# Delta-rule attention ahead of two expert layers: whole-tile key loads, side-by-side key copies on ScalarE, key masks behind the first solve, all late evictions on ScalarE

## The chip, the cores and the metric

One core of a Trainium2 chip runs the whole program. The metric is the device time of one execution in microseconds (us), lower is better. TensorE (PE) multiplies matrices, VectorE (DVE), ScalarE (ACT) and GpSimd (POOL) work elementwise, SyncE (SP) issues most of the transfers. TensorE's granted clock is 1.00 or 0.50 of full speed (2.4 or 1.2 GHz) in every row of a single stretch; a stretch that mixes both shows a value between.

## The reference, cut to what matters

```python
def _attn_ref(q, k, v, beta):            # (2, 8, 768, 48), beta (2, 8, 768)
    k_n = k / (np.linalg.norm(k, axis=-1, keepdims=True) + 1e-06)
    state = np.zeros((B, H, D, D))
    for t in range(S):
        y[:, :, t] = einsum('bhd,bhde->bhe', q[:, :, t], state)
        v_old = einsum('bhde,bhd->bhe', state, k_n[:, :, t])
        state = state + beta_t * einsum('bhd,bhe->bhde', k_n[:, :, t], v[:, :, t] - v_old)
...
    x = attn_out.transpose(0, 2, 1, 3).reshape(B * S, H * D)     # 1536 x 384
    x = _moe_ref(x=x, **moe_kwargs)        # top-1 expert of 8, 384 -> 1024 -> 384, relu
    return _moe2_ref(x=x, **moe2_kwargs)   # a second such layer, with an output gate
```

The attention has a state that each token changes. The two expert layers behind it send every token through one of eight experts.

## The kernel before

The 768 tokens of each of the 16 heads are cut into 24 chunks of 32 tokens (`NCH`), and four chunks make a group (`NQ` = 6). The work on all heads of a chunk goes together. A chunk's tokens act on one another through a triangular system, so its inverse is needed before the state can take the chunk in. `inlane` (L588) makes the inverses for a batch of chunks at once, one step per row of the triangle: `BATCH` is 4, 4, 8 and 8 chunks. The batches are called solve 1 to 4 below. Solves 1, 3 and 4 run on DVE (a product L706 and a subtraction L708 per step: 15 such pairs in solve 1, 31 in solves 3 and 4), solve 2 on POOL.

A solve begins with the Gram products of its chunks (`gram`, L524; matmuls L543 for group 0, L537 for the others) in halves `h` of two chunks. L537 has a key tile `kq` as one operand and, as the other, a tile `kb` in which the keys of the two batch halves stand side by side with zeros between. Before, both are loaded from memory: `load_k` (L447) loads `kq` of groups 1 to 5 in two transfers of 48 partitions, into tiles that DVE and ACT have set to zero (L1073 to L1079), and `load_kb` (L461) loads the same numbers again, twice 48 partitions, into `kb`, which POOL has set to zero (L1070). Each half of a Gram product has a PSUM buffer of the ring `R` (two buffers), which is read twice: by ACT for the solve (L560, `Ge`, into `Gs`) and by DVE for the mask of the query part (L566, `Pe`, into `PT`), and is free for the next user after both.

After a solve its result is spread into `zt` by DVE (L747), ACT (L745) and transfers (L749). In solves 1 and 2 the chunks are corrected by `fix` (L772): matmul f1 (L782), transposition on DVE (L786), matmul f2 (L793), four ACT evictions (L798). Then the recurrence runs, `step(c)` (L822), with these matmuls in each chunk: AT (L835), U (L845), AS (L850), QS (L864), DS (L870), PW (L885). AS needs the state of the chunk before it. From AS on the chain goes: four evictions of `wpd` (L857 on ACT or L855 on DVE), DS, two evictions of the state `sbd` (L878 on ACT or L876 on DVE), AS of the next chunk. Chunks 0 to 15 evict on ACT, chunks 16 to 23 in turn on ACT and DVE (`WENG`, `SENG`, L900). `logits` and `route` follow the chunks, and the expert layers follow the attention.

No engine chooses its order on the chip. `Plan` (L221) sorts all operations of the attention by estimated times and ranks and writes one fixed order per engine; an instruction that waits holds all that stand behind it on its engine. `keep_warm` (L380) adds matmuls without use (`warm`, L820) where the planner thinks TensorE too idle to keep its clock; `NW0` (L1122) more stand at the start. Loads go out on SP in the order of the list in L1060.

```python
        add(("Ge", q, h), "A", 0.38, lambda h=h: e1(h), ((hd, 1),) + ...
        add(("Pe", q, h), "V", 0.5, lambda h=h: e2(h), ((hd, 1), "bl") + ...
        WENG, SENG = ("AAAA", "AA") if c < 16 else ("AVAV", "VA")
```

Of the kernel before, what the change touches and what calls it, by code (L numbers as in the profile page):

```python
# [7 lines left out]
F32 = mybir.dt.float32  # L8
# [212 lines left out]
class Plan:  # L221
# [169 lines left out]


def attention(tc, ctx, con, I, C, wg, A, xt1, xa1, xt2, zr, T1, Ti1, place, load_w, late, wts, xb, new_x, gather):
# [6 lines left out]
    starts = [sum(BATCH[:i]) for i in range(NB)]  # L400
    bof = lambda c: max(j for j in range(NB) if starts[j] <= c)
    pl = Plan()
    pl.bufs.update(Lt=1, Zt=1, kb=2, kq=10, kt=4, vt=3, PT=5, R=2, WA=2, O=1, ATn=2, pay=4, lgs=2, Gs=1, Bl=3, z=1, ztmp=1, xTs=1, sq=1, f1s=4, Gw=2)
    P = 4.3
    GP = 0.0021
    add = pl.add
    rest = lambda c: (NCH - c) * P
# [12 lines left out]
    kbb = [big.tile([128, 2, 2, 8, 64], F32, name=f"kb{i}") for i in range(2)]  # L420
    wab = [ps.tile([128, 512], F32, name=f"WA{i}") for i in range(2)]
    Sps = ps.tile([128, 2, 4, 48], F32, name="Sps")
    zps = ps.tile([128, 512], F32, name="zps")
    T, st = {}, {}
    GR = ((0, 1), (2, 3), (4,), (5,))
    gof = {q: g[0] for g in GR for q in g}
# [16 lines left out]
    def chain(key, xfer, f, new=None, uses=(), n=1, deps=()):  # L443
        dma(key, xfer, f, deps, behind=order[-1:], new=new, uses=uses, n=n)
        order.append(key)

    def load_k(q, h):  # L447
        i = slice(2 * h, 2 * h + 2)

        def f(e):  # L450
            t = T["kqt", q, h] = kqb[(2 * q + h) % len(kqb)]
            src = I["kq"][:, 4 * q + i.start : 4 * q + i.stop]
            if q == 0:
                e.dma_start(t, src)
# [4 lines left out]
        chain(("kq", q, h), 1.46 if q == 0 else 1.1, f, new=("kq", ("kqt", q, h)), n=2 if q else 1, deps=(("kz", 2 * q + h),) if 2 <= 2 * q + h < len(kqb) else ())

    def load_kb(q, h):  # L461
        def f(e):
            t = T["kbt", q, h] = kbb[(2 * q + h) % 2]
            src = I["kq"][:, 4 * q + 2 * h : 4 * q + 2 * h + 2]
            for b in range(2):
                e.dma_start(t[64 * b : 64 * b + 48, b], src[64 * b : 64 * b + 48])

        chain(("kb", q, h), 1.1, f, new=("kb", ("kbt", q, h)), n=2, deps=(("bz", h),))

    def load_kt(q, h):  # L470
        i = slice(2 * h, 2 * h + 2)
# [52 lines left out]
    def gram(q, pri=0.0):  # L524
# [37 lines left out]
        def e2(h):  # L562
            if h == 0:
                sb("PT", ("PT", q), [128, 4, 2, 2, 32])
            x, y = parts(h, T["PT", q], 32, 64)
            nc.vector.tensor_tensor(x, y, bl[:, NB].unsqueeze(1).to_broadcast([128, 8, 32]), ALU.mult)  # L566

        for h in range(2):
            hd = ("G", q, h)
            for i in range(2):  # L570
                dp = (("kq", q, h), ("kb", q, h)) if q else (("kq", 0, i),)
                if i:
                    dp += ((hd, 0),)
                elif h:
                    dp += ((("G", q, 0), 1),)
                elif q:
                    dp += ((("G", q - 1, 1), 1),)
                us = (("kqt", q, h), ("kbt", q, h)) if q else (("kqt", 0, i),)
                add((hd, i), "P", 0.4 if q else 0.32, lambda h=h, i=i: mm(h, i), dp, pri, behind=late_, uses=us + ((hd,) if i else ()), new=None if i else ("R", hd))
        for h in range(2):  # L580
            hd = ("G", q, h)
            f0 = starts[b] // 4
            f = q == f0 and h == 0
            add(("Ge", q, h), "A", 0.38, lambda h=h: e1(h), ((hd, 1),) + (() if f else (("Ge", f0, 0),)), pri, uses=(hd,) + (() if f else (("Gs", b),)), new=("Gw" if BATCH[b] == 4 else "Gs", ("Gs", b)) if f else None)
            add(("Pe", q, h), "V", 0.5, lambda h=h: e2(h), ((hd, 1), "bl") + ((("Pe", q, 0),) if h else ()), rest(4 * q + 2 * h) + 12, lp=500.0, uses=(hd,) + ((("PT", q),) if h else ()), new=None if h else ("PT", ("PT", q)))
    ZV = {}

    def inlane(bi):  # L588
# [13 lines left out]

        def z0():
            if psum:
                d["z"] = zps[:, 0:256].rearrange("p (i m) -> p i m", m=16)
            elif blk:
                d["z"] = zzb[:, 0:256].rearrange("p (i m) -> p i m", m=16)
            else:
                d["z"] = sb("z", Z, [128, 32, 32])
            (nc.vector if psum else nc.gpsimd).memset(d["z"], 0.0)  # L610
# [211 lines left out]
    def step(c):  # L822
# [246 lines left out]
    for i in range(2):
        add(("bz", i), "G", 1.9, lambda i=i: nc.gpsimd.memset(kbb[i], 0.0), lp=600.0 - i)  # L1070
    for i, (n, t) in enumerate([("zta0", zt8[:, 0:4]), ("wpd0", wpd[0]), ("sbd1", sbd[1]), ("wpd1", wpd[1]), ("zta1", zt8[:, 4:8]), ("sbd0", sbd[0])]):
        add(n, "G", {"zta0": 1.9, "zta1": 1.9}.get(n, 0.7), lambda t=t: nc.gpsimd.memset(t, 0.0), pri=500 - i)
    for n, (k, t) in enumerate([("Sz", Sps), ("Wz0", wab[0]), ("Wz1", wab[1])] + [(("kz", i), kqb[i]) for i in range(2, len(kqb))]):  # L1073
        kd = n > 2
        if n > 5:
            f = lambda t=t: nc.scalar.activation(t.rearrange("p a b c -> p (a b c)"), nc.const_aps.tensor(0.0, [128, 1024], F32), AF.Copy)
        else:
            f = lambda t=t: nc.vector.memset(t, 0.0)
        add(k, "A" if n > 5 else "V", 1.08 if kd else 0.5, f, pri=1200 - n, after=0.0)  # L1079
# [34 lines left out]
    for j in range(2):  # L1114
# [664 lines left out]
```

## Time and profile before

| | us |
|---|---|
| three runs, median | 553.44 |
| three runs, lowest and highest | 550.39, 555.61 |
| the profiled execution, its time | 550.83 |
| the profiled execution, its span | 549.0 |
| granted TensorE clock over the span | 0.931 of full speed |

The span runs from the first to the last profiled instruction; 1.83 us of the execution lie outside it. Times of rows are counted from the start of the span. The attention ends at about 194.4 us, where the last table for the gathers is written, and the expert layers take the rest. A row of the timeline gives start, duration, engine, line, operation, tiles, count, and in brackets how long the engine had been idle before it and what ended that.

### The profile page before, as it was taken

Reading aid. Unit: us, or ns where it says so; the run is one execution under the profiler, and the core shown is the slowest. Engines: PE = TensorE matmul, PEld = TensorE weight load, DVE = VectorE, ACT = ScalarE, POOL = GpSimd, SP = SyncE. Lnnn points to the kernel's source line nnn. Section 1 sums busy time; section 2 is a strip of 40 time slices with the busy share of each in tenths; the row PEclk is TensorE's granted clock in tenths of the full one; section 3 lists DMA queues with packets and bytes.
Section 4 is the critical chain, followed back from the end, with each engine's and each line's share of the span. In section 5 each row is a group of like instructions: output and inputs, shape, how many; then the busy total and the mean of one; then the engine's idle time right before and its main releaser. Section 6 shows DMA issues by size and latency. Waiting matters only on the chain. (4 is left out here: it accounts for less than half of the span.)

```text
span 549.0 us, 13219 instructions
## 1 busy us (share of the span) xinstructions
PE 482.5 (88%) x5173; PEld 412.8 (75%) x5182; DVE 355.6 (65%) x1042; ACT 275.0 (50%) x597; POOL 136.5 (25%) x161
## 2 busy tenths in 40 slices
PE   8798989799899869999999999999788996898780
PEld 3357767677676539999999999988677895898570
DVE  6566656899255466788788788987236853466550
ACT  6014635646744435675665656644225651445540
POOL 8504100000000055053254141116331513121111
PEclk9896958859999979999999999999999999799897
DMA  8992170353646122857547676433932844335400
GB/s 253 249 241 43 36 213 27 80 153 91 174 111 184 32 63 61 304 180 256 179 130 276 206 233 219 137 88 82 348 98 84 299 176 154 143 99 192 146 11 14
DMA packets 56538, 83.21 MB, mean 152 GB/s; under 512 B 15615, under 2 KB 38359, under 8 KB 56432
## 3 DMA queue, kind: packets, MB, share of 16 engines
q1 hardware_dynamic: 50688, 69.90, 41.8%
q0 software_dynamic: 5744, 11.95, 7.1%
q8 instruction: 59, 0.97, 0.7%
q14 instruction: 47, 0.39, 0.2%
HBM read 72.80 MB, written 11.72 MB: 154 GB/s over the span
## 5 line engine op out<-in xcount | busy, mean ns | idle before, releaser
L1177 DVE TENSOR_TENSOR l<-r,h 128x768 fp32r<-128x768 f32 x128 | 118.1, 952 | 14.8 <-ACT h L1173 12.0
L1173 ACT ACTIVATE h<-r 128x768 fp32r<-128x768 f32 x128 | 101.8, 837 | 3.5 <-DMA xa<-aux 3.5
L1189 PE MATMUL hp<-xh,h 128*128 128x256 f32 x288 | 84.4, 293 | 13.4 <-issue 8.8
L1189 PE MATMUL y<-h,hh 128*128 128x384 f32 x240 | 84.4, 352 | 0.0
L1191 PE MATMUL hp<-xl,h 128*128 128x256 f32 x288 | 81.9, 284 | 0.0
L1190 PE MATMUL hp<-xh,l 128*128 128x256 f32 x288 | 81.8, 284 | 0.0
L1190 PE MATMUL y<-h,hl 128*128 128x384 f32 x240 | 80.9, 337 | 0.0
L1191 PE MATMUL y<-l,hh 128*128 128x384 f32 x240 | 80.7, 336 | 0.0
L1221 ACT ACTIVATE hh<-hp 128x256 fp32r<-128x256 f32 x96 | 36.5, 384 | 67.6 <-PE hp L1191 57.2
L1224 DVE SCALAR_TENSOR_TENSOR hl<-hp,hh 128x256 fp32r<-128x256 f32 x96 | 39.7, 421 | 45.3 <-ACT hh L1221 41.0
L1189 PEld LDWEIGHTS hp<-xh,h 128*128 128x128 f32 x288 | 55.8, 194 | 15.4 <-issue 13.2
L1190 PEld LDWEIGHTS hp<-xh,l 128*128 128x128 f32 x288 | 56.1, 195 | 0.1
L1191 PEld LDWEIGHTS hp<-xl,h 128*128 128x128 f32 x288 | 55.7, 193 | 0.1
L168 POOL DMA_INDIRECT out<-fo,fix x19 | 21.6, 1134 | 109.3 <-DVE fo L1401 77.6
L1190 PEld LDWEIGHTS y<-h,hl 128*128 128x128 f32 x240 | 45.3, 189 | 0.7 <-issue 0.4
L1189 PEld LDWEIGHTS y<-h,hh 128*128 128x128 f32 x240 | 45.2, 188 | 0.0
L1191 PEld LDWEIGHTS y<-l,hh 128*128 128x128 f32 x240 | 45.1, 188 | 0.0
L168 POOL DMA_INDIRECT xt<-p,rix x16 | 16.6, 1036 | 101.6 <-ACT h L1173 72.4
L210 POOL DMA_INDIRECT xb<-xt,Ti x32 | 38.1, 1191 | 12.6 <-issue 6.1
L857 ACT ACTIVATE wpd<-WA 32x192 f32<-32x192 f32 x80 | 25.8, 322 | 18.0 <-PE WA L850 11.1
L1203 ACT ACTIVATE xh<-xp 128x384 fp32r<-128x384 f32 x29 | 14.3, 492 | 40.4 <-PE xp L1200 28.4
L820 PE MATMUL warm<-const-bfloat16-1.0 128*128 128x512 bf16 x93 | 29.0, 444 | 1.4 <-PEq L1772 0.8
(273 smaller groups left out, 881.8 us busy)
## 6 DMA issues: line engine op xcount, KB each, us to landing
r<-moe_w SPq DMA_DIRECT2D x64, 768.0 KB
kq<-kq SPq DMA_DIRECT2D x20, 192.0 KB
kb<-kq SPq DMA_DIRECT2D x20, 192.0 KB
xt<-zr SPq DMA_DIRECT2D x3, 776.0 KB
kt<-ktm SPq DMA_DIRECT2D x12, 192.0 KB
vt<-vtm SPq DMA_DIRECT2D x6, 384.0 KB
xt<-pay SPq DMA_DIRECT2D x16, 96.0 KB
kq<-kq SPq DMA_DIRECT2D x2, 512.0 KB
```

The lines of the kernel that those rows point to most:

```text
L168: i = nc.gpsimd.indirect_dma_start(out=dst, out_offset=IO(ap=idx, axis=0), in_=src, in_offset=None, bounds_check=rows - 1, oob_is_err=False)
L210: nc.gpsimd.indirect_dma_start(out=dst, out_offset=None, in_=src, in_offset=IO(ap=ix, axis=0), bounds_check=1536, oob_is_err=False)
L820: nc.tensor.matmul(t, one_[:, 0:128], one_, start=True, stop=True)
L857: nc.scalar.activation(wp[p, :, Q, :], st["W", c][p], AF.Copy)
L1173: nc.scalar.activation(v(h), v(r), AF.Copy)
L1177: nc.vector.tensor_tensor(v(l), v(r), v(h).bitcast(F32), ALU.subtract)
L1189: nc.tensor.matmul(o, lh, rh, start=first, stop=False)
L1190: nc.tensor.matmul(o, ll, rh, start=False, stop=False)
L1191: nc.tensor.matmul(o, lh, rl, start=False, stop=last)
L1203: nc.scalar.activation(xs()[0][:, :, s], p[0], AF.Copy)
L1221: nc.scalar.activation(hs()[0][:, f], p[0], AF.Relu)
L1224: nc.vector.scalar_tensor_tensor(hs()[1][:, f], p[0], 0.0, hs()[0][:, f].bitcast(F32), ALU.max, ALU.subtract)
```

## The change

```diff
     def keep_warm(self, free, t, d, u):
         k, t0 = 0, t
+        if t < 24:
+            return 0
...
-    pl.bufs.update(Lt=1, Zt=1, kb=2, kq=10, kt=4, vt=3, PT=5, R=2, ...
+    pl.bufs.update(Lt=1, Zt=1, kb=2, kq=10, kt=4, vt=3, PT=5, R=3, ...
+    KA, KL = 3, (0.0, 900.0, 0.0, 0.0)
+    LOADS = "k0 l t0 v0 k1 t1 v1 k2 t2 k3 v2 t3 k4 K4 k5 K5 v3 t4 v4 t5 v5"
...
-    zps = ps.tile([128, 512], F32, name="zps")
...
-            src = I["kq"][:, 4 * q + i.start : 4 * q + i.stop]
-            if q == 0:
-                e.dma_start(t, src)
+            e.dma_start(t, I["kq"][:, 4 * q + i.start : 4 * q + i.stop])
+
+        chain(("kq", q, h), 1.4, f, new=("kq", ("kqt", q, h)))
+
+    def load_kb(q, h):
+        def f(b, e=None):
+            if b == 0:
+                T["kbt", q, h] = kbb[(2 * q + h) % 2]
+            t, p = T["kbt", q, h], slice(64 * b, 64 * b + 48)
+            if e:
+                e.dma_start(t[p, b], I["kq"][p, 4 * q + 2 * h : 4 * q + 2 * h + 2])
             else:
-                for p in (0, 64):
-                    e.dma_start(t[p : p + 48], src[p : p + 48])
...
+                nc.scalar.activation(t[p, b], T["kqt", q, h][p], AF.Copy)
...
+        if q > KA:
+            chain(("kb", q, h), 1.7, both, new=("kb", key), n=2, deps=((("G", q if h else q - 1, 0 if h else 1), 0),))
+        else:
...
+                add(("kb", q, h, b), "A", 0.95, lambda b=b: f(b), (("kq", q, h), ("bz", h)) + ...
...
-            add(("Pe", q, h), "V", 0.5, lambda h=h: e2(h), ((hd, 1), "bl") + ((("Pe", q, 0),) if h else ()), ...
+            add(("Pe", q, h), "V", 0.5, lambda h=h: e2(h), ((hd, 1), "bl") + ((("Pe", q, 0),) if h else (("il", 0, "zt"),) if q else ()), ...
...
-                d["z"] = zps[:, 0:256].rearrange("p (i m) -> p i m", m=16)
+                d["z"] = wab[1][:, 0:256].rearrange("p (i m) -> p i m", m=16)
...
-        WENG, SENG = ("AAAA", "AA") if c < 16 else ("AVAV", "VA")
+        WENG, SENG = "AAAA", "AA"
...
-    for x in 'k0 l t0 v0 k1 K1 t1 v1 k2 K2 t2 v2 k3 K3 t3 k4 K4 v3 t4 k5 K5 v4 t5 v5'.split():
+    for x in (LOADS + "".join(f" K{q}" for q in range(1, KA + 1))).split():
...
-    for n, (k, t) in enumerate([("Sz", Sps), ("Wz0", wab[0]), ("Wz1", wab[1])] + [(("kz", i), kqb[i]) for i in range(2, len(kqb))]):
...
+    for n, (k, t, dp) in enumerate([("Sz", Sps, ()), ("Wz0", wab[0], ()), ("Wz1", wab[1], (("il", 0, "zz1"),))]):
...
-    NW0 = 13
+    NW0 = 11
```

All `kq` loads are one transfer of 128 partitions, whose padding comes from memory, so the eight zero fills of `kq` are gone. `kb` of groups 1 to 3 is filled by twelve ACT copies of 48 partitions (two per half); groups 4 and 5 still load it. The masks of groups 1 to 5 wait for the transposition that ends solve 1. Solve 1 works in the PSUM buffer `WA1` instead of one of its own, which lets the ring `R` have three buffers, and the zero fill of `WA1` stands behind solve 1. All chunks evict on ACT. The planner puts no matmuls without use before its own time 24, and eleven instead of thirteen stand at the start. The planner's orders change with all that. Line numbers of the code rise by 5 to 10.

On DVE at the start of solve 1 (`zps` is its system, `ztmp` a product, PT the mask of a Gram half) there stood before:

```order
L697 COPY zps<-lc 128x16
L706 TENSOR_TENSOR ztmp<-zps,r_96 128x15
L566 TENSOR_TENSOR PT<-R,bl 128x256
L708 TENSOR_TENSOR zps<-zps,ztmp 128x15
L706 TENSOR_TENSOR ztmp<-zps,r_96 128x28
L708 TENSOR_TENSOR zps<-zps,ztmp 128x14x2
L706 TENSOR_TENSOR ztmp<-zps,r_96 128x39
L566 TENSOR_TENSOR PT<-R,bl 128x256
```

On DVE at the end of solve 1 there stands now:

```order
L716 TENSOR_TENSOR ztmp<-WA_111,r_96 128x15
L718 TENSOR_TENSOR WA_111<-WA_111,ztmp 128x15
L740 TENSOR_SCALAR r_97<-WA_111,bl 128x16x16 x2
L745 STREAM_TRANSPOSE r_96<-r_97 128x16x2x16
L757 COPY zt_86<-r_96 32x8x32 x2
L576 TENSOR_TENSOR PT<-R,bl 128x256 x3
L780 STREAM_TRANSPOSE r_94<-r_97 128x512
L576 TENSOR_TENSOR PT<-R,bl 128x256
L628 STREAM_TRANSPOSE r_96<-r_298 128x512
L576 TENSOR_TENSOR PT<-R,bl 128x256
```

The four masks that stood between the thirty steps of solve 1 now stand behind the spreading of its result.

On ACT, from the square of the keys of group 0 on (`ls` is the square root that solve 1 needs), there stood before:

```order
L494 ACTIVATE r_243<-kt 128x768
L560 ACTIVATE r_222<-R 128x8x32
L502 ACTIVATE s_276<-n_250 128x16
L635 ACTIVATE ls_270<-ln_273 128x16
L560 ACTIVATE r_332<-R 128x256 x2
L560 ACTIVATE Gs<-R 128x256 x2
L745 ACTIVATE zt_86<-r_96 32x8x32 x2
```

and there stands now:

```order
L504 ACTIVATE r_223<-kt 128x768
L570 ACTIVATE r_201<-R 128x8x32
L512 ACTIVATE s_243<-n_231 128x16
L467 ACTIVATE kb_108<-kq_100 48x1024
L645 ACTIVATE ls_236<-ln_239 128x16
L467 ACTIVATE kb_108<-kq_100 48x1024
L467 ACTIVATE kb_109<-kq_101 48x1024 x2
L570 ACTIVATE r_298<-R 128x256
L467 ACTIVATE kb_108<-kq_102 48x1024
```

One copy has come in front of `ls`; by the spreading of solve 1 ten of the twelve have been issued.

On PE, from U of chunk 4 to DS of chunk 4 (`kq_98` and `kq_99` are the keys of group 5), there stood before:

```order
L845 MATMUL WA_110<-vt,zt_86 128x48 x4
L850 MATMUL WA_110<-sbd_89,ATn 32x96 x8
L537 MATMUL R<-kb_108,kq_98 32x128 x16
L782 MATMUL R<-r_332,zt_86 128x32 x4
L835 MATMUL WA_111<-zt_86,kt 48x128 x4
L537 MATMUL R<-kb_109,kq_99 32x128 x16
L870 MATMUL Sps<-wpd_87,kt 48x192 x4
```

and there stands now:

```order
L855 MATMUL WA_110<-vt,zt_86 128x48 x4
L860 MATMUL WA_110<-sbd_89,ATn 32x96 x8
L803 MATMUL R<-r_95,r_94 16x16 x16
L874 MATMUL O<-sbd_89,kq_100 32x96 x8
L547 MATMUL R<-kb_108,kq_98 32x128 x16
L855 MATMUL WA_111<-vt,zt_86 128x48 x4
L880 MATMUL Sps<-wpd_87,kt 48x192 x4
```

The second Gram half of group 5 has left the place between AS and DS of chunk 4; it now stands one chunk later.

## Rows read from the trace of the kernel before

**Rows 1.** Windows by stage: length, busy time of each engine, granted clock, transfers.

```profile
core 0: us, PE busy (x) PEld busy (x) DVE busy (x) ACT busy (x) POOL busy (x), PEclk, DMA share, GB/s
0.00:43.30 43.30, 35.70 (x476) 17.62 (x482) 26.44 (x79) 13.75 (x26) 19.24 (x33) 0.92 1.00 246
43.30:105.30 62.00, 55.08 (x1069) 42.58 (x1058) 41.68 (x112) 34.02 (x103) 9.08 (x31) 0.77 0.28 73
144.90:194.40 49.50, 44.15 (x890) 32.23 (x892) 23.27 (x101) 24.37 (x62) 0.00 (x0) 1.00 0.37 95
```

**Rows 2.** Waits of DVE from 16.3 to 33.3 us: total, times, longest.

```profile
DVE PT L566 <- ACT Gs L560: 5.5, 2, 4.2
DVE PT L566 <- ACT r L560: 2.9, 2, 1.4
```

**Rows 3.** Windows of the solve steps alone (`ztmp`), solves 1, 3, 4: length, DVE busy.

```profile
16.30:33.30 17.00, 6.24 (x30) 0.81 1.06 246
59.80:100.50 40.70, 21.00 (x62) 0.79 0.37 98
110.80:136.45 25.65, 21.22 (x62) 0.79 0.42 116
```

**Rows 4.** Timeline of DVE around the end of solve 1.

```profile
29.01 0.42 DVE L566 TENSOR_TENSOR PT<-R,bl 128x256 f32<-128x256 f32 x1 [4.22 <-ACT Gs L560]
...
33.03 0.18 DVE L708 TENSOR_TENSOR zps<-zps,ztmp 128x15 f32<-128x15 f32 x1
...
35.23 0.59 DVE L747 COPY zt<-r 32x256 f32<-32x256 f32 x2
```

**Rows 5.** Windows as in rows 1, of whole-tile loads and of 48-partition loads.

```profile
3.00:8.00 5.00, 4.94 (x46) 1.90 (x46) 2.57 (x4) 4.98 (x6) 5.00 (x5) 1.00 1.02 371
...
28.00:42.00 14.00, 12.48 (x180) 7.08 (x176) 9.56 (x29) 2.63 (x8) 0.00 (x0) 0.94 1.06 235
```

**Rows 6.** Timeline of ACT: five zero fills, and `ls` of solve 1.

```profile
2.03 4.84 ACT L1076 ACTIVATE kq<-const-float32-0.0 128x1024 f32<-128x1024 f32 x5
...
13.09 0.22 ACT L635 ACTIVATE ls<-ln 128x16 f32<-128x16 f32 x1 [1.50 <-DVE ln L629]
```

**Rows 7.** Timeline of PE: matmuls without use, a Gram half, f1 and U of chunk 0.

```profile
0.78 6.47 PE L820 MATMUL warm<-const-bfloat16-1.0 128*128 128x512 bf16 x17 [0.78 <-PEq L1772]
...
30.77 3.45 PE L820 MATMUL warm<-const-bfloat16-1.0 128*128 128x512 bf16 x14
...
38.35 1.08 PE L537 MATMUL R<-kb,kq 128*32 128x128 f32 x32
39.36 0.85 PE L782 MATMUL R<-r,zt 128*128 128x32 f32 x6
...
43.31 1.09 PE L845 MATMUL WA<-vt,zt 128*128 128x48 f32 x8
```

**Rows 8.** Waits of DVE from 59.8 to 100.6 us.

```profile
DVE PT L566 <- ACT Gs L560: 7.8, 3, 4.4
```

**Rows 9.** Windows as in rows 1, of a stretch at the lower clock.

```profile
104.70:121.80 17.10, 16.42 (x170) 12.34 (x172) 13.92 (x43) 7.09 (x20) 0.00 (x0) 0.50 0.63 160
```

**Rows 10.** Timeline of PE: AS of chunks 8, 9, 12, 15, 16 and 23.

```profile
109.42 0.87 PE L850 MATMUL WA<-sbd,ATn 128*32 128x96 f32 x16
...
117.80 0.87 PE L850 MATMUL WA<-sbd,ATn 128*32 128x96 f32 x16
...
132.62 0.54 PE L850 MATMUL WA<-sbd,ATn 128*32 128x96 f32 x16
...
144.88 0.54 PE L850 MATMUL WA<-sbd,ATn 128*32 128x96 f32 x16 [0.68 <-ACT sbd L878]
...
151.50 0.52 PE L850 MATMUL WA<-sbd,ATn 128*32 128x96 f32 x16
...
183.47 0.54 PE L850 MATMUL WA<-sbd,ATn 128*32 128x96 f32 x16
```

**Rows 11.** Waits from 150 to 187 us.

```profile
ACT wpd L857 <- DVE wpd L855: 5.1, 11, 1.1
```

More of the change, by code (lines that the diff above doesn't have):

```diff
@@ L402, in attention @@
     pl = Plan()
-    pl.bufs.update(Lt=1, Zt=1, kb=2, kq=10, kt=4, vt=3, PT=5, R=2, WA=2, O=1, ATn=2, pay=4, lgs=2, Gs=1, Bl=3, z=1, ztmp=1, xTs=1, sq=1, f1s=4, Gw=2)
+    pl.bufs.update(Lt=1, Zt=1, kb=2, kq=10, kt=4, vt=3, PT=5, R=3, WA=2, O=1, ATn=2, pay=4, lgs=2, Gs=1, Bl=3, z=1, ztmp=1, xTs=1, sq=1, f1s=4, Gw=2)
     P = 4.3
+    KA, KL = 3, (0.0, 900.0, 0.0, 0.0)
+    LOADS = "k0 l t0 v0 k1 t1 v1 k2 t2 k3 v2 t3 k4 K4 k5 K5 v3 t4 v4 t5 v5"
     GP = 0.0021
@@ L451, in f, with both @@
             t = T["kqt", q, h] = kqb[(2 * q + h) % len(kqb)]
-            src = I["kq"][:, 4 * q + i.start : 4 * q + i.stop]
-            if q == 0:
-                e.dma_start(t, src)
-            else:
-                for p in (0, 64):
-                    e.dma_start(t[p : p + 48], src[p : p + 48])
[L459 to L464, printed above, removed]
+            e.dma_start(t, I["kq"][:, 4 * q + i.start : 4 * q + i.stop])
[7 more added lines that the diff above has]
+                e.dma_start(t[p, b], I["kq"][p, 4 * q + 2 * h : 4 * q + 2 * h + 2])
+            else:
+                nc.scalar.activation(t[p, b], T["kqt", q, h][p], AF.Copy)
+        def both(e):
+            f(0, e)
+            f(1, e)
+        key = ("kbt", q, h)
+        if q > KA:
+            chain(("kb", q, h), 1.7, both, new=("kb", key), n=2, deps=((("G", q if h else q - 1, 0 if h else 1), 0),))
+        else:
             for b in range(2):
-                e.dma_start(t[64 * b : 64 * b + 48, b], src[64 * b : 64 * b + 48])
-        chain(("kb", q, h), 1.1, f, new=("kb", ("kbt", q, h)), n=2, deps=(("bz", h),))
+                add(("kb", q, h, b), "A", 0.95, lambda b=b: f(b), (("kq", q, h), ("bz", h)) + ((("kb", q, h, 0),) if b else (("kb", q, 0, 1),) if h else (("kb", q - 1, 1, 1),) if q > 1 else ()), lp=KL[q], uses=(("kqt", q, h),) + ((key,) if b else ()), new=None if b else ("kb", key))
     def load_kt(q, h):
@@ L570, in gram @@
             for i in range(2):
-                dp = (("kq", q, h), ("kb", q, h)) if q else (("kq", 0, i),)
+                dp = (("kq", q, h),) + ((("kb", q, h),) if q > KA else (("kb", q, h, 0), ("kb", q, h, 1))) if q else (("kq", 0, i),)
                 if i:
@@ L584, in gram @@
             add(("Ge", q, h), "A", 0.38, lambda h=h: e1(h), ((hd, 1),) + (() if f else (("Ge", f0, 0),)), pri, uses=(hd,) + (() if f else (("Gs", b),)), new=("Gw" if BATCH[b] == 4 else "Gs", ("Gs", b)) if f else None)
-            add(("Pe", q, h), "V", 0.5, lambda h=h: e2(h), ((hd, 1), "bl") + ((("Pe", q, 0),) if h else ()), rest(4 * q + 2 * h) + 12, lp=500.0, uses=(hd,) + ((("PT", q),) if h else ()), new=None if h else ("PT", ("PT", q)))
+            add(("Pe", q, h), "V", 0.5, lambda h=h: e2(h), ((hd, 1), "bl") + ((("Pe", q, 0),) if h else (("il", 0, "zt"),) if q else ()), rest(4 * q + 2 * h) + 12, lp=500.0, uses=(hd,) + ((("PT", q),) if h else ()), new=None if h else ("PT", ("PT", q)))
     ZV = {}
@@ L1072, in attention @@
         add(n, "G", {"zta0": 1.9, "zta1": 1.9}.get(n, 0.7), lambda t=t: nc.gpsimd.memset(t, 0.0), pri=500 - i)
-    for n, (k, t) in enumerate([("Sz", Sps), ("Wz0", wab[0]), ("Wz1", wab[1])] + [(("kz", i), kqb[i]) for i in range(2, len(kqb))]):
[L1074 to L1079, printed above, removed]
+    for n, (k, t, dp) in enumerate([("Sz", Sps, ()), ("Wz0", wab[0], ()), ("Wz1", wab[1], (("il", 0, "zz1"),))]):
+        add(k, "V", 0.5, lambda t=t: nc.vector.memset(t, 0.0), dp, pri=1200 - n if n < 2 else 0.0)
     for q in range(NQ):
```

## The prediction

> **What bounds the kernel now.** I read the windows by stage first [rows 1]. In the expert layers, behind 194.4 us, the built order of PE and DVE is the same before and after, so their time is carried over whole; everything is decided in the attention. Up to 43.3 us the transfer queues are full (share 1.00) and no chunk has started. From 43.3 to 105.3 us, chunks 0 to 7, PE is busy for 55.1 of 62.0 us, but at a granted clock of 0.77: it is slow rather than short of work. Chunks 16 to 23 run at 1.00.
>
> In the head the chain runs through DVE. The waits of DVE during solve 1 [rows 2] and the windows of its steps [rows 3] say the same twice: 17.00 us for steps that are busy for 6.24, because four masks stand between the steps and wait 5.5 + 2.9 = 8.4 us for Gram halves whose keys have not come. Solve 3 shows the same sickness: 40.70 us for 21.00 us of steps, where solve 4 needs 25.65 for 21.22 [rows 3]. Chunk 8 cannot start before solve 3 ends. From chunk 9 on the bound is the loop AS, evictions, DS, evictions, AS: (144.88 - 132.62) / 3 = 4.09 us a chunk [rows 10].
>
> **The change part by part.** I work against the profiled 550.83 us (span 549.0 and 1.83 around it).
>
> Solve 1. Take the four masks away: 17.00 - 8.4 - 4 x 0.42 [rows 2 to 4] = 6.9 us. It then ends 10.1 us earlier, at 33.21 - 10.1 = 23.1, if it starts when it did. It starts when ACT has made `ls` (13.09, after 1.50 us of idleness) [rows 6]. A copy now stands ahead of `ls`. The nearest row is a fill of as many elements per partition, 4.84 / 5 = 0.97 us [rows 6]. It delays `ls` only if its keys land after 13.09 - 0.97 = 12.1 us. Ahead of and in them are 2.4 MB by the shapes; in the first 8 us some 2.1 MB came (371 GB/s from 3 us on [rows 5]), so they are there by about 9 to 11 us, whichever rate follows. Cost 0. Five ACT fills and three DVE fills that go stood in front of a wait for the first keys: gain 0 to 1, I take 0.
>
> Loads. While whole tiles came, the queues moved 371 GB/s; while 48-partition pieces came, 235, at the same full share [rows 5]. Groups 1 to 3 need 1.05 MB each in place of 4 x 2 x 0.2 = 1.57 MB, so at the whole-tile rate a group takes 2.8 us, where it took 6.7. The first half of group 2 is 4.3 MB into the list: at 371 GB/s about 14 us, at 235 about 17, and I add 2 for landing. The copies (two of 0.97 a half) and the Gram evictions share ACT, so that Gram half is done at about 20 us, 22 at the slow rate.
>
> What is late next. The masks keep the three buffers of `R`, so the second half of group 2 has to wait for the first mask. The copies of solve 1's result ended 35.82 - 33.21 = 2.6 us after its last step [rows 4]: 23.1 + 2.6 + 0.42 = 26.1 us. On PE 26 matmuls without use stand ahead of that half. At full clock they cost 3.45 / 14 = 0.246 us each, in the cold start 6.47 / 17 = 0.38 [rows 7]: 6.4 to 9.9 us, so they end between 26.4 and 32. I take 28.4, between, because PE has had little to do since 6 us. Then come that half with seven more such matmuls (1.08 + 7 x 0.246 = 2.8) and a half of group 3 (1.1): f1 of chunk 0 at 32.3. From f1 to U took 43.31 - 39.36 = 3.95 us [rows 7]; a Gram half is now in between and most of that stretch's matmuls without use are not, so 4.2: U at 36.5, against 43.31. The head gives 6.8 us, 3.3 with the slow matmuls at the far end and 8.8 at the near one.
>
> The Trainium skill, page "TensorE: Matmul & The Clock Gate", section "What's actually happening", says that the throttled state is the default and that activity releases it, which speaks against taking matmuls without use out of the start. The trace agrees in the first row of the group named above: 0.38 us for each there, 0.246 later. By that rule the far end of the range would hold.
>
> Zero fill of `WA1`. It now stands on DVE behind the transposition for solve 3; AT of chunk 1 waits for it, and U and AS of chunk 1 stand behind AT on PE. I cost it at 0, because AT also stands behind DS of chunk 0, which needs four evictions first. If DVE is late there, it eats from the next term.
>
> Chunks 0 to 7 and solve 3. The end that excludes any further gain carries the 6.8 us to chunk 8. The other end lets solve 3 run as solve 4 does: 40.70 - 25.65 = 15.05 more, 21.8 in all. Of the excess, 7.8 us are waits for the masks of groups 4 and 5 [rows 8]. I take these as gone: the last mask stands five steps later in solve 3, one Gram half has left the place between AS and DS of chunk 4, and the keys of group 5 are no longer behind a queue that is full to 43 us. The rest (the ending of solve 2 on DVE, the transpositions between) stays. Together 14.6 us at chunk 8.
>
> Chunks 8 to 15. 109.42 to 144.88 is 35.5 us [rows 10], with 17.1 us at clock 0.50 in front [rows 9]; at 4.09 us a chunk it would be 28.6. So the change is worth 0 to 6.8 here. I take 0: chunk 8 again starts behind a PE that has waited for solve 3, as it did when the clock fell.
>
> Chunks 16 to 23. (183.47 - 151.50) / 7 = 4.57 us a chunk against 4.09 where ACT evicts alone [rows 10]: 7 x 0.48 = 3.4 us at best. ACT waited 5.1 us for DVE there [rows 11], so the two engines took turns and did not share. Against it: ACT was busy 24.4 of 49.5 us [rows 1] and gets about half as much again, in a fixed order with the evictions of the logits; I bound that at a loss of 2. I take +2.0, towards the neighbouring chunks.
>
> Sum: 14.6 + 0 + 2.0 = 16.6; 550.83 - 16.6 = 534.2 us. The median of the runs before lies 2.6 us above the profiled one, and I forecast a median: 537 us.
>
> **The rivals.**
> A. The clock stays up. If PE reaches chunk 8 without a long wait, chunks 8 to 15 give their 6.8, and some 2 more come out of solve 3: 553.4 - 25.4 = 528 us. For it: solve 3 no longer lags by 15 us. Against: the clock fell in three places before, and no matmuls without use were put into these.
> B. Only a late head. The 26 matmuls run cold and the masks of groups 4 and 5 wait as before: 3.3 + 2.0, 548 us. For it: the masks' Gram halves still hang on loads of 48 partitions that now wait for earlier Gram halves.
> C. Slower: the lower clock through the recurrence. The price is in two rows: chunk 8 to 9 took 117.80 - 109.42 = 8.38 us cold, against 4.09, so each us at 0.50 costs 0.51 us. Before, about 28 us (0.77 over 62.0 us [rows 1]) and 17.1 us [rows 9] were at 0.50. It decides from 16.6 / 0.51 = 33 us more on; with 43 us more, nearly all of chunks 0 to 15, the time is 559 us. For it: 34 fewer matmuls without use ahead of U of chunk 0, counted in the orders. Against: 26 in one block stand right ahead of the recurrence.
> D. The loads are no faster, since what slowed them was not the 48 partitions. Group 2 is ready 3 us later, the head gives 3.8, and the sum is 13.6: 540 us. Against it: both rows of the loads are at a full share.
>
> **How the numbers follow.** Forecast 0.50, A 0.22, B 0.13, C 0.06, D 0.09. About 1% is what a measurement of this kernel can tell from no change, that is 5.5 us. The forecast, A and D lie below that, 0.81; B about on it, 0.13 within; C above, 0.06. The low end takes all the upper bounds, 21.8 + 6.8 + 3.4 = 32: 521 us. The high end reaches past B, 549 us. That leaves out C and little else, and no more than 2 in 10.
>
> **What would show it.** Right: no mask between the steps of solve 1, which ends near 23 us; above 340 GB/s until the keys of group 3 are in; U of chunk 0 at 34 to 40 us; solve 3 in about 33 us; AS of chunk 8 near 95 us; AS of chunks 16 to 23 spaced at 4.1 to 4.4 us; the expert layers as long as before. Wrong: `ls` or the spreading of solve 1 waiting behind key copies on ACT, PE held ahead of the second half of group 2 until past 32 us, or a clock of 0.50 over more than 70 us between U of chunk 0 and chunk 15.

## The result, and the profile after

| | before | after |
|---|---|---|
| median, four runs each on one chip, us | 551.91 | 522.13 |
| lowest and highest, us | 548.0, 555.61 | 521.87, 525.09 |
| ratio, 95% interval | | 0.9474 (0.9395 to 0.9552) |
| second set of runs: median of 11 and of 6 runs, us | 548.01 | 524.75 |
| ratio there, 95% interval | | 0.9627 (0.9567 to 0.9687) |
| profiled execution, us | 550.83 | 521.87 |

The kernel is faster by about 4 to 5%. The forecast was 537 us in a range of 521 to 549; the measured 522.13 lies 1 us above the low end, nearer to rival A's 528 than to the forecast. Ratios are formed from undisturbed runs of each kernel alone, so they can lie nearer to 1 than the medians do. Profile against profile the gain is 28.96 us, where I had summed 16.6. Line numbers are ten higher than before in the attention and five higher in the expert layers.

The windows by stage of the kernel after, to lay beside [rows 1] (length, busy time of the engines, granted clock, transfers):

```profile
0.00:33.25 33.25, 25.55 (x416) 14.82 (x417) 22.95 (x74) 20.12 (x32) 19.43 (x33) 0.90 0.81 281
33.25:81.90 48.65, 45.79 (x1094) 35.12 (x1094) 41.43 (x114) 32.86 (x103) 9.66 (x31) 1.00 0.36 95
81.90:114.00 32.10, 30.56 (x658) 23.26 (x658) 29.49 (x83) 23.30 (x63) 0.00 (x0) 1.00 0.67 186
114.00:161.70 47.70, 45.05 (x891) 32.23 (x891) 16.22 (x91) 32.30 (x84) 0.00 (x0) 1.00 0.41 103
161.70:520.10 358.40, 314.54 (x2096) 296.55 (x2096) 232.95 (x658) 180.92 (x345) 108.90 (x97) 0.95 0.49 160
```

The second row is the one to look at: chunks 0 to 7 take 48.65 us instead of 62.00, at a granted clock of 1.00 instead of 0.77. From U of chunk 0 to the end of the attention no stretch is at 0.50, where before three were (10.2, 17.1 and 17.1 us: 44.4 in all). The third is in [rows 9]; the first two, and the expert layers, in the kernel before:

```profile
46.70:56.90 10.20, 10.20 (x173) 8.31 (x176) 4.48 (x13) 3.63 (x13) 7.10 (x26) 0.50 0.01 2
70.50:87.60 17.10, 15.83 (x199) 12.05 (x202) 7.95 (x21) 5.60 (x19) 0.00 (x0) 0.50 0.68 188
194.40:549.00 354.60, 310.00 (x2096) 292.14 (x2096) 233.21 (x658) 180.45 (x345) 108.19 (x97) 0.97 0.49 162
```

The timeline of PE, its AS rows as in [rows 10], and U of chunk 0 as in [rows 7]:

```profile
33.25 1.06 PE L855 MATMUL WA<-vt,zt 128*128 128x48 f32 x8
...
84.09 0.54 PE L860 MATMUL WA<-sbd,ATn 128*32 128x96 f32 x16
...
114.04 0.54 PE L860 MATMUL WA<-sbd,ATn 128*32 128x96 f32 x16 [0.68 <-ACT sbd L888]
...
120.59 0.54 PE L860 MATMUL WA<-sbd,ATn 128*32 128x96 f32 x16
...
151.89 0.54 PE L860 MATMUL WA<-sbd,ATn 128*32 128x96 f32 x16 [0.48 <-ACT sbd L888]
```

These are U of chunk 0 and AS of chunks 8, 15, 16 and 23. Each set against its row before gives the gain reached at that point, and the differences say where it came from:

| stretch | gain forecast, us | gain measured, us |
|---|---|---|
| up to U of chunk 0 | 6.8 | 43.31 - 33.25 = 10.06 |
| to AS of chunk 8 | 7.8 | 25.33 - 10.06 = 15.27 |
| to AS of chunk 15 | 0 | 30.84 - 25.33 = 5.51 |
| to AS of chunk 23 | 2.0 | 31.58 - 30.84 = 0.74 |
| to the end of the attention (194.4, 161.7) | 0 | 32.7 - 31.6 = 1.1 |
| expert layers | 0 | 354.6 - 358.4 = -3.8 |

In the solves, the windows of the steps as in [rows 3] (length, DVE busy):

```profile
14.00:21.50 7.50, 6.28 (x30) 0.89 1.04 397
44.00:78.00 34.00, 21.31 (x62) 1.00 0.49 130
86.80:112.40 25.60, 21.20 (x62) 1.00 0.73 205
```

Solve 1 has no waits between its steps any more: 7.50 us in place of 17.00. Solve 3 takes 34.0 in place of 40.7. The waits of DVE from 44 to 78 us, as in [rows 8], fell from 7.8 to 3.5 us:

```profile
DVE PT L576 <- ACT Gs L570: 3.5, 2, 2.5
```

The windows of the loads, as in [rows 5]:

```profile
3.00:8.00 5.00, 4.42 (x135) 2.34 (x133) 0.77 (x2) 0.72 (x2) 5.00 (x5) 1.00 1.00 376
8.00:16.00 8.00, 3.34 (x64) 2.84 (x64) 6.95 (x22) 6.59 (x10) 7.20 (x14) 0.57 1.04 405
16.00:26.00 10.00, 8.42 (x86) 4.03 (x78) 9.13 (x31) 7.10 (x10) 4.76 (x10) 1.00 0.89 321
```

At the same full share 405 GB/s came where 235 came before, and from 16 us on the share is below 1: the queues run dry. A quarter of a whole key tile is padding, though (32 of 128 partitions, by the shapes), so of 405 GB/s of key tiles about 304 would be keys (an estimate).

### The profile page after: what moved, and what is told of

It is laid out like the page before. It is cut to its first block, busy times and chain, and to the rows that moved or that the text cites. A ratio compares the mean times of both kernels' runs of the same rounds, so it can differ in the third digit from the quotient of the medians.

```text
span 520.1 us, 13133 instructions
## 1 busy us (share of the span) xinstructions
PE 461.5 (89%) x5154; PEld 402.0 (77%) x5154; DVE 343.0 (66%) x1016; ACT 289.5 (56%) x626; POOL 138.0 (27%) x161
## 3 DMA queue, kind: packets, MB, share of 16 engines
q1 hardware_dynamic: 50080, 68.85, 41.5%
## 5 line engine op out<-in xcount | busy, mean ns | idle before, releaser
L1182 DVE TENSOR_TENSOR l<-r,h 128x768 fp32r<-128x768 f32 x128 | 118.0, 952 | 12.4 <-ACT h L1178 9.5
L1195 PE MATMUL hp<-xh,l 128*128 128x256 f32 x288 | 83.0, 288 | 4.7 <-issue 4.7
L1196 PEld LDWEIGHTS hp<-xl,h 128*128 128x128 f32 x288 | 56.9, 198 | 0.2 <-DVE xl L1211 0.2
L1194 PEld LDWEIGHTS y<-h,hh 128*128 128x128 f32 x240 | 45.2, 188 | 0.0
L168 POOL DMA_INDIRECT xt<-p,rix x16 | 16.6, 1038 | 101.6 <-ACT h L1178 73.9
L867 ACT ACTIVATE wpd<-WA 32x192 f32<-32x192 f32 x96 | 30.9, 322 | 9.4 <-PE WA L860 5.9
L1194 PE MATMUL hp<-h,xh 128*128 128x512 f32 x42 | 20.2, 480 | 12.6 <-issue 9.0
```

The lines of the kernel that those rows point to most:

```text
L168: i = nc.gpsimd.indirect_dma_start(out=dst, out_offset=IO(ap=idx, axis=0), in_=src, in_offset=None, bounds_check=rows - 1, oob_is_err=False)
L867: nc.scalar.activation(wp[p, :, Q, :], st["W", c][p], AF.Copy)
L1182: nc.vector.tensor_tensor(v(l), v(r), v(h).bitcast(F32), ALU.subtract)
L1194: nc.tensor.matmul(o, lh, rh, start=first, stop=False)
L1195: nc.tensor.matmul(o, ll, rh, start=False, stop=False)
L1196: nc.tensor.matmul(o, lh, rl, start=False, stop=last)
```

## The experiments

Two theories stood at the start. "Clock": a good part of the gain behind U of chunk 0 is TensorE's clock, which no longer falls in the recurrence. "Waits": the earlier keys and the moved masks do it all, and the clock only fills time in which the chain waits anyway. Beside these, each part of the change had to be told from the others. The table has every run; its columns are the median (lowest to highest), the ratio to the kernel before, and from the profile U of chunk 0, the end of the attention, and the us at clock 0.50 between the two.

| kernel | median, us | ratio (95%) | U of chunk 0 | attention ends | at 0.50 |
|---|---|---|---|---|---|
| before | 548 to 553 in four sets of runs | 1 | 43.3 | 194.4 | 44.4 |
| after | 522.13 (521.87 to 525.09) | 0.947 (0.940 to 0.955) | 33.3 | 161.7 | 0 |
| after_again | 524.75 (521.86 to 528.24) | 0.963 (0.957 to 0.969) | 36.1 | 163.8 | 0 |
| ev_old | 521.45 (516.80 to 524.16) | 0.951 (0.933 to 0.969) | 35.6 | 164.1 | 0 |
| mask_old | 521.16 (516.64 to 523.62) | 0.949 (0.935 to 0.962) | 38.2 | 167.7 | 3.4 |
| mask_again | 522.19 (520.76 to 524.44) | 0.958 (0.953 to 0.963) | 37.8 | 167.0 | 3.8 |
| nowarm | 524.63 (522.80 to 525.06) | 0.952 (0.949 to 0.956) | 31.9 | 165.0 | 13.7 |
| after_warm | 523.18 (519.15 to 524.81) | 0.952 (0.948 to 0.956) | 33.8 | 161.8 | 0 |
| kq_pieces | 526.84 (526.51 to 529.98) | 0.967 (0.960 to 0.974) | 39.4 | 171.4 | 10.2 |
| before_load | 530.09 (521.76 to 536.86) | - | 36.4 | 171.4 | 10.2 |
| before_mask | 538.04 (534.51 to 541.61) | 0.976 (0.969 to 0.982) | 45.2 | 180.9 | 6.8 |
| kb_mem | 538.64 (534.22 to 541.13) | 0.989 (0.982 to 0.996) | 38.7 | 179.7 | 13.7 |
| load_old | 540.50 (537.80 to 545.15) | 0.989 (0.975 to 1.004) | 42.5 | 178.8 | 6.8 |
| before_warm | 543.21 (538.18 to 548.42) | 0.991 (0.985 to 0.997) | 43.5 | 184.4 | 6.8 |

**The clock alone** (before_warm). Nothing is moved; 27 matmuls without use go into places where PE waited.

```diff
     for t, e, end, o in seq:
...
+        dummy({("f1", 2): 6, ("DS", 3): 2, ("rq", 0, ("tr", 3)): 5, ("AS", 7): 3, ("DS", 7): 4, ("AT", 8): 7}.get(o["key"], 0))
         o["fn"](e) if isinstance(o["dur"], dict) else o["fn"]()
```

> Before, with 27 matmuls without use set ahead of instructions on which TensorE waited before the three low-clock stretches of the recurrence (f1 of chunk 2, DS and a transposition in chunk 3, AS, DS of chunk 7 and AT of chunk 8); orders otherwise unchanged. Theory 'clock' (the lower clock itself cost about 14 us: 5.6 from U of chunk 0 to solve 3, 2.9 behind solve 3, 5.5 in chunks 8 to 15): less than 15 us at 0.50 between 40 and 150 us, time 538 to 546. Rival 'waits' (the clock only filled time in which the chain waited for VectorE): the clock stays up, and the time is 549 to 555 all the same.

The median fell by 9.6 us against the 552.77 of the kernel before in the same set of runs; by the ratio it is 0.3 to 1.5%. Its windows by stage (chunks 0 to 7, 8 to 15, the rest of the attention) show how:

```profile
43.30:101.00 57.70, 51.42 (x1107) 38.62 (x1107) 41.13 (x113) 32.60 (x101) 9.41 (x31) 0.94 0.32 79
101.00:135.40 34.40, 31.57 (x661) 23.39 (x660) 30.79 (x86) 23.57 (x65) 0.00 (x0) 1.00 0.64 173
135.40:184.40 49.00, 44.12 (x890) 32.26 (x892) 24.71 (x110) 24.34 (x62) 0.00 (x0) 1.00 0.40 102
```

The clock of chunks 0 to 7 rose from 0.77 to 0.94, U of chunk 0 stayed where it was (43.5), and the attention ended 10.0 us earlier, although DVE still waited 8.5 us for masks in solve 3:

```profile
DVE PT L566 <- ACT Gs L560: 8.5, 3, 5.5
```

So 37.6 us less at 0.50 gave 10.0 us, 0.27 us for each, net of what the 27 matmuls cost. "Clock" holds, "waits" falls as the whole cause. The plain runs of the kernel before point the same way: over 31 of them the mean granted clock goes from 0.911 to 0.949, and a straight line through their times gives 0.27 to 0.34 us for each us at 0.50, depending on which of them are taken. That is a correlation and no trial.

**The loads undone, and the loads alone** (load_old, before_load). Keys in pieces into zeroed tiles, `kb` from memory, and the list as it was; and the reverse in the kernel before. In load_old, and in kb_mem and kq_pieces below, the zero fill of `WA1` got a higher rank, since the planner else holds AT of chunk 1 back for it.

```diff
-            e.dma_start(t, I["kq"][:, 4 * q + i.start : 4 * q + i.stop])
...
+            if q == 0:
+                e.dma_start(t, src)
+            else:
+                for p in (0, 64):
+                    e.dma_start(t[p : p + 48], src[p : p + 48])
...
+            for b in range(2):
+                e.dma_start(t[64 * b : 64 * b + 48, b], src[64 * b : 64 * b + 48])
```

> After, with the loads of before: keys in 48-partition pieces into zeroed tiles, side-by-side keys from memory, the old list of loads; the masks stay behind solve 1. Theory 'loads': 235 to 250 GB/s again and queues full past 38 us, U of chunk 0 at 38 to 42, a low clock somewhere in the recurrence, time 532 to 545. Rival 'masks': solve 1 still ends near 23, U of chunk 0 by 36, time 524 to 530.

> Before, with the loads of the change alone: whole-tile keys, copies of groups 1 to 3 on ScalarE, the new list; the masks stay between the steps of solve 1, the late evictions are shared as before. Theory 'loads' (they carry nearly all): transfers above 340 GB/s until the keys of group 3 are in, attention ends at 163 to 171 us, time 522 to 531. Rival 'both needed' (the masks between the steps hold the head back all the same): VectorE waits above 5 us in solve 1, attention ends past 175, time 533 to 545.

load_old lost 18 us of the gain, as "loads" had it, although solve 1 ended at 22.2 us there, as "masks" had it. The timeline of PE shows the place: the first half of group 2 stands 6.90 us for `kb` and ends at 27.8, where after it is done by 18.8.

```profile
25.90 1.94 PE L540 MATMUL R<-kb,kq 128*32 128x128 f32 x32 [6.90 <-DMA kb<-kq]
28.17 6.53 PE L823 MATMUL warm<-const-bfloat16-1.0 128*128 128x512 bf16 x23 [0.33 <-issue]
```

before_load, with the loads alone, came to 530.09, 20 us below the 550.56 of the kernel before beside it, and ended the attention at 171.4, where the whole change ends it at 161.7 and 163.8. Its runs spread by 15 us, so the size is rough. DVE still waited 3.7 us for masks between the steps of solve 1 there, which took 12.4 us: less than "both needed" had expected, more than after.

**Which part of the loads** (kb_mem, kq_pieces). Each undoes one half of it; kb_mem also takes the old list of loads, and kq_pieces the zero fills.

```diff
-                nc.scalar.activation(t[p, b], T["kqt", q, h][p], AF.Copy)
+                e.dma_start(t[64 * b : 64 * b + 48, b], src[64 * b : 64 * b + 48])
```

> After, with the side-by-side keys loaded from memory again in 48-partition pieces (old list, no ScalarE copies), the keys themselves still as whole tiles. By the rows a group is 1.05 MB at 371 GB/s plus 0.79 MB at 235: 6.2 us, against 2.8 in after and 6.7 in before. Theory 'copies' (what the loads gain is that the second reading of the keys is gone): second half of group 2 ready past 23 us, U of chunk 0 at 40 to 43, time 535 to 543. Rival 'whole tiles' (the shape of the transfer is what gains): U of chunk 0 by 36, time 523 to 529.

```diff
-            e.dma_start(t, I["kq"][:, 4 * q + i.start : 4 * q + i.stop])
...
+                for p in (0, 64):
+                    e.dma_start(t[p : p + 48], src[p : p + 48])
```

> After, with the keys of groups 1 to 5 in two pieces of 48 partitions each into zeroed tiles again, the side-by-side copies still by ScalarE. By the rows a group is 0.79 MB at 235 GB/s: 3.3 us, against 2.8. Theory 'copies': U of chunk 0 at 33 to 36, attention ends by 165, time 521 to 526. Rival 'whole tiles': U of chunk 0 past 38, time 530 to 538.

With `kb` from memory the time is 538.64, nearly that of load_old, and U of chunk 0 at 38.7 ("copies" had said 40 to 43); the same Gram half waits 5.14 us for it:

```profile
23.00 0.44 PE L535 MATMUL R<-kb,kq 128*32 128x128 f32 x4 [5.14 <-DMA kb<-kq]
```

With `kq` in pieces it is 526.84. From 8 to 16 us the pieces, with two loads of `kt` among them, came at 250 GB/s, with the share full, against 405 of whole tiles:

```profile
8.00:16.00 8.00, 1.94 (x32) 1.51 (x32) 6.13 (x18) 6.26 (x12) 6.44 (x10) 0.65 1.06 250
```

Against after_again in the same set of runs, kb_mem loses 13.9 us and kq_pieces 2.1; the attention ends 15.9 and 7.5 us later. So the second reading of the keys, which the copies replace (with the list that goes with it), is the larger part, and the shape of the transfer the smaller: 0.79 MB a group at 250 GB/s take 3.2 us, 1.05 MB at 405 take 2.6 (an estimate by these rates). In kq_pieces both expectations held in part: U of chunk 0 came where "whole tiles" had put it, at 39.4, and the time near that of "copies", though the attention ended past its 165. Its planner had put 33 matmuls without use ahead of the second half of group 2, seven more than after, and U hangs on them too (below).

**The masks** (mask_old, mask_again, before_mask).

```diff
-            add(("Pe", q, h), "V", 0.5, ..., ((hd, 1), "bl") + ((("Pe", q, 0),) if h else (("il", 0, "zt"),) if q else ()), ...
+            add(("Pe", q, h), "V", 0.5, ..., ((hd, 1), "bl") + ((("Pe", q, 0),) if h else ()), ...
```

> After, with the masks of groups 1 to 5 free to stand between the steps of solve 1 again; loads, copies and evictions stay. Theory 'loads' (the masks waited only because the keys came late, and now they come early): VectorE waits for Gram halves in solve 1 fall from 8.4 to under 3 us, U of chunk 0 at 34 to 37, time 523 to 527. Rival 'masks' (moving the masks is what frees solve 1 whatever the loads do): waits stay above 5 us, U of chunk 0 past 39, time 530 or more.

> The kernel with the masks between the steps of solve 1 a second time, beside the changed kernel on one chip. Theory 'masks are worth 4 to 6 us in the head' (as the end of the attention at 167.7 against 161.7 says): 4 to 6 us slower than the changed kernel. Rival (what they cost in the head is made good later): within 2 us of it.

> Before, with the masks of groups 1 to 5 behind solve 1 alone (three buffers of R, solve 1 in WA1, whose zero fill stands early on VectorE); loads and late evictions as before. Theory 'loads': solve 1 ends near 23 us and nobody can use it, since the keys of group 2 and 3 still come over a full queue; U of chunk 0 at 41 to 44, time 539 to 551. Rival 'masks': U of chunk 0 by 37, time 528 to 538.

In before_mask the edit is the reverse, with `R=3` and solve 1 in `WA1` as in the change.

Masks back between the steps of solve 1 do cost the head something: waits of 4.4 us there (between "loads", under 3, and "masks", above 5), U of chunk 0 at 38.2 and 37.8, the attention ending 3 to 6 us later. The waits of mask_old:

```profile
DVE PT L576 <- PE R L547: 4.4, 4, 1.9
```

And yet both medians, 521.16 and 522.19, are no worse than those of the changed kernel (522.13, 524.75). The expert layers, whose order on PE and DVE is the same, took 354.1 and 353.0 us there, against 358.4 and 358.7. PE's waits for which the profile shows no cause do not explain it: they come to 14.6 us in after_again and, at other places, to 14.5 in mask_again. These waits of PE in the expert layers, after_again first:

```profile
PE hp L1194 <- issue: 11.9, 4, 4.8
PE hp L1195 <- issue: 2.7, 1, 2.7
...
PE hp L1194 <- issue: 10.9, 5, 4.7
PE hp L1196 <- issue: 3.6, 2, 3.1
```

What differs there is the clock: after_again has 38.1 us at 0.50 in these layers, mask_again 27.9. Why it falls more in the one than in the other was not tried. The theory "masks" fell in both directions: with early keys moving them is seen at the end of the attention and not in the time; and alone, with late keys, it gave 12.5 us (538.04 against 550.56) without bringing the head forward at all. U of chunk 0 came at 45.2, later than before; what went was the clock's fall, 6.8 us at 0.50 instead of 44.4, and a part of solve 3 (35.8 us). Neither expectation held: the time lies on the border of their ranges, and U of chunk 0 in neither. Its planner had put 20 matmuls without use ahead of the second half of group 2, which I did not take apart from the masks.

**The evictions** (ev_old).

```diff
-        WENG, SENG = "AAAA", "AA"
+        WENG, SENG = ("AAAA", "AA") if c < 16 else ("AVAV", "VA")
```

> After, with the evictions of chunks 16 to 23 in turn on ScalarE and VectorE again. Theory (the evictions are worth almost nothing, because ScalarE, now the only evicting engine, becomes the place where AS waits): AS of chunks 16 to 23 spaced at 4.5 us as in both traces, time 521.5 to 524. Rival (they give the 2.0 us forecast, and something else hides it in the comparison): spacing 4.7 or more, 524 to 526 us.

From AS of chunk 16 to AS of chunk 23 it took 153.59 - 122.14 = 31.45 us:

```profile
122.14 0.54 PE L860 MATMUL WA<-sbd,ATn 128*32 128x96 f32 x16
...
153.59 0.54 PE L860 MATMUL WA<-sbd,ATn 128*32 128x96 f32 x16
```

After: 151.89 - 120.59 = 31.30. The evictions are worth 0.2 us. The theory's reason was not right either: what AS waits for is shown by the timeline of chunk 22 in the kernel after.

```profile
148.01 1.36 ACT L867 ACTIVATE wpd<-WA 32x192 f32<-32x192 f32 x4
...
148.84 0.54 PE L874 MATMUL O<-sbd,kq 128*32 128x96 f32 x16
...
149.31 0.64 PE L943 MATMUL R<-cst,pay 128*96 128x128 f32 x4
...
149.88 0.86 PE L880 MATMUL Sps<-wpd,kt 128*48 128x192 f32 x8
```

ACT's four evictions end there at 148.01 + 1.36 = 149.37, and DS starts at 149.88, when the transpositions of the logits (L943) ahead of it are about through. In this chunk it is PE's own order that holds DS, not the evictions.

**The matmuls without use** (nowarm, after_warm).

```diff
-            dummy(o)
+            dummy(0 if 15 < t < 90 else o)
```

> After, without the 44 matmuls without use that stand from the second Gram half of group 2 to DS of chunk 1; all else in the same order. Theory 'clock' (TensorE keeps its full clock through the recurrence because it enters it busy): the Gram halves and U of chunk 0 run at 0.50, over 15 us at 0.50 between 15 and 85 us, the attention ends past 165, time 524 to 535. Rival 'ballast' (the loads alone feed TensorE, and these matmuls only delay f1 of chunk 0): U of chunk 0 at 29 to 32, attention ends by 161, time 516 to 521.

U of chunk 0 came 1.3 us earlier ("ballast"), then the clock fell from 35.4 to 49.1 us ("clock"), and the attention ended 3.3 us later. The time, 524.63, cannot be told from that of the changed kernel. So these 44 matmuls are not what made the change. U itself ran at full clock, against the expectation; the fall came behind it:

```profile
35.40:49.10 13.70, 13.70 (x222) 10.14 (x222) 8.51 (x27) 6.11 (x20) 8.49 (x30) 0.50 0.12 36
```

```diff
-    ev(-15.9, lambda: warm(9))
+    ev(-15.9, lambda: warm(25))
```

> After, with 16 more matmuls without use at the start of the expert layers, where TensorE waits 3 us and the clock falls for 6.8 us in every trace so far (at 200 us before, at 169 us after). Theory 'clock': that stretch goes, the first expert's products run at 0.12 us each instead of 0.21, 2 to 3 us less to their end, time 518 to 521. Rival 'queue' (the wait is for a branch that comes after these matmuls, so it moves with them): products start 2 to 3 us later, no gain, 521 to 525.

"Queue" was right, as the timeline of PE at the start of the expert layers shows: the 33 matmuls end at 168.0, and PE then waits 2.97 us, as it had waited 3.06 behind 17.

```profile
162.43 5.58 PE L1552 MATMUL y<-const-bfloat16-1.0,cb 128*128 128x384 bf16 x33
170.98 0.84 PE L1205 MATMUL xp<-cst,xb 128*128 128x128 f32 x6 [2.97 <-PEq L1593]
```

The wait comes with a branch behind them and was not filled from in front. The clock behind it fell for 3.4 us in place of 6.8, which gave back 0.9 of the 2.6 us by which the products started later. No gain that the time shows: 523.18.

**The same kernel again** (after_again).

> The changed kernel a second time, for its spread: 521 to 524, attention ends at 161 to 164 us, no clock of 0.50 between U of chunk 0 and the end of the attention. If the clock falls there in this profile, its absence in the first was chance, and the theory 'clock' loses its row.

The clock stayed at 1.00 through the recurrence in this profile too. The head did not repeat: U of chunk 0 at 36.08 instead of 33.25. The block of matmuls without use ahead of the second half of group 2 is the difference. In the first profile:

```profile
18.76 5.86 PE L830 MATMUL warm<-const-bfloat16-1.0 128*128 128x512 bf16 x26
24.57 0.64 PE L547 MATMUL R<-kb,kq 128*32 128x128 f32 x16
```

In the second, with the clock at 0.50 from 10.0 to 23.6 us:

```profile
20.14 7.32 PE L830 MATMUL warm<-const-bfloat16-1.0 128*128 128x512 bf16 x25 [0.33 <-issue]
27.40 0.64 PE L547 MATMUL R<-kb,kq 128*32 128x128 f32 x16
```

## Why the prediction was right in direction and short in size

**Solve 1 and the loads: right.** Solve 1 shortened by 9.5 us (17.00 to 7.50; I had 10.1), it ended at 21.4 us (I had 23.1; `ls` came 2.0 us earlier than I had allowed), and whole tiles ran at 376 to 405 GB/s (I had 371). The copies did not hold `ls` up: on ACT it comes right behind the first, at 11.04 instead of 13.09, and each takes 1.06 us (I had 0.97). They do stand in the way of the Gram halves, as I had counted: the first half of group 2 waits 1.58 us for its second copy.

```profile
9.97 1.06 ACT L467 ACTIVATE kb<-kq 48x1024 f32<-48x1024 f32 x1 [0.23 <-DMA kq<-kq]
11.04 0.22 ACT L645 ACTIVATE ls<-ln 128x16 f32<-128x16 f32 x1
...
17.74 1.08 PE L547 MATMUL R<-kb,kq 128*32 128x128 f32 x32 [1.58 <-ACT kb L467]
```

Rival D is gone with this.

**The head, 6.8: the mechanism right, the size too small.** The step was "I take 28.4, between" for the end of the 26 matmuls. They ended at 24.6 in one profile, outside my bounds of 26.4 to 32, and at 27.4 in the other, inside them; the head gave 10.06 and 7.2 us against bounds of 3.3 to 8.8. In the first they began at 18.8 us, 1.2 earlier than I had, and ran at full clock throughout, where I had taken the middle because PE had had little to do; the first mask, the other thing that the half behind them waits for, was done at about 24.5. The Trainium skill, page "TensorE: Matmul & The Clock Gate", section "What's actually happening", says that the number of matmuls at the lower clock, from the start, varies from run to run of one kernel. The two profiles show such a spread later in the head: the clock came back to 1.00 at 15.7 us in one and at 23.6 in the other, and the block took 0.225 and 0.293 us a matmul.

**Chunks 8 to 15, 0: wrong.** The step that failed is "chunk 8 again starts behind a PE that has waited for solve 3, as it did when the clock fell". It did wait, and nearly as long: 0.80 us at DS of chunk 7 and 0.96 at AT of chunk 8, against 0.83 and 1.52 before. The last two rows are of the kernel before.

```profile
79.60 0.86 PE L880 MATMUL Sps<-wpd,kt 128*48 128x192 f32 x8 [0.80 <-ACT wpd L867]
80.39 0.55 PE L895 MATMUL O<-wpd,PT 128*32 128x48 f32 x32
81.90 1.08 PE L845 MATMUL WA<-zt,kt 128*48 128x128 f32 x16 [0.96 <-ACT zt L755]
...
102.52 0.86 PE L870 MATMUL Sps<-wpd,kt 128*48 128x192 f32 x8 [0.83 <-ACT wpd L857]
105.38 1.95 PE L835 MATMUL WA<-zt,kt 128*48 128x128 f32 x16 [1.52 <-ACT zt L745]
```

The clock stayed up behind it, and through chunks 8 to 15 of all the other profiles but for 3.4 us at chunk 15 in mask_old. I had taken one fall in one profile for a property of the place. Rival A, whose 6.8 us this is, measured 5.5; but its condition, a PE that reaches chunk 8 without a long wait, is hardly nearer than before, so why the clock stayed up here is not shown.

**Chunks 0 to 7, 7.8 beyond the head: wrong in its reason and half in size.** I had taken the masks' waits in solve 3 as gone and carried everything else over. The waits gave 4.3 us (7.8 to 3.5). What I had left out is in the first row that I quoted: a granted clock of 0.77. Solve 3 began 16.6 us after U of chunk 0 before and 10.9 after; before, 10.2 us at 0.50 lay in between. At the 0.27 us that before_warm gave for each us at 0.50, the 44.4 us that are gone make some 12 of the 21 us that chunks 0 to 15 gave beyond the head. My price of 0.51, from two chunks at 0.50 in which PE was the bound, is too high here; that this is because DVE's solve is the bound was not tried.

**The evictions, 2.0: mis-sized.** 0.2 us by ev_old, 0.7 by the two traces. The turns that ACT and DVE took were real, but DS then waited for PE's own order.

**The expert layers, carried over whole: off by 3.8.** The step was "their time is carried over whole". In thirteen profiles of the same order they took 352.7 to 358.9 us, and this goes with their own clock: the six profiles above 357 us have 36.8 to 41.5 us at 0.50 there, the seven up to 355.2 us have 24.5 to 34.0. The kernel before has 24.5, the one after 36.8; at 0.27 us each the difference would be 3.3 of the 3.8 (an estimate). So it seems that a part of what the clock gave in the recurrence was lost again behind it; what makes it fall there was not tried.

**The sum.** Head +3.3, chunks 0 to 7 +7.5, chunks 8 to 15 +5.5, the end of the attention +1.1, evictions -1.3 and expert layers -3.8 are 12.3 more than forecast, which is the distance of 16.6 to 28.96. Of the signs that I had named, AS of chunk 8 came at 84.1 us instead of near 95, and AS of chunks 16 to 23 stood 4.47 us apart instead of 4.1 to 4.4. That the time still lies in the range is partly luck: up to chunk 8 the gain was 25.3 us, past the 21.8 that I had set as the most, and the evictions and the expert layers, each short of its term, took it back. Rival B (548) and C (559) fell; C's cause was brought about in nowarm, for 13.7 us (C needed 33), and the time stayed within 2.5 us of the changed kernel's. Which of the loads and the clock "made" the gain can't be split without rest: the loads alone give about 20 us, the masks alone 12.5, the clock alone 5 to 10, and all together 23 to 30, because each of the first two also ends most of the clock's fall.

## What to carry over

Read the granted clock of each stage before pricing its waits: a stage in which PE is busy at 0.77 has a gain in it that no list of waits shows, and filling PE's waits with matmuls without use is a cheap way to see how much. Undo each part of a compound change by itself and do it alone: the moved masks, the plainest part of this one, gave nothing that the time shows once the keys came early. And look for data that is read twice: copies on an engine with time to spare, in place of a second load, were the largest single part.

## What had not been expected

The same program's clock and head differ from one profile to the next (33.25 and 36.08 us at U of chunk 0), so a term of 2 to 3 us in the head can't be told from one profile. Stretches with transfers of 48 partitions ran at 250 GB/s, and with 128 alone at 405, with the queues' share full in both. The Trainium skill, page "DMA: Bandwidth & Descriptors", section "Rules for kernel authors", asks for one transfer of 128 partitions in place of two to disjoint halves. The traces agree by these rates, though with its padding counted out a whole key tile would bring about 304 (an estimate). And the expert layers, in one and the same order, vary by 6 us together with the time that they spend at 0.50. PE waits there up to 8.2 us (in the kernel before) for nothing that the profile shows; that stays open.
